# A second accumulator bank for every other pair of heads in the first chunk, and the start's step list written anew

## The chip, the cores and the metric

The kernel runs on one core of a Trainium2 chip. The metric is device time of one execution in microseconds (us); the smaller the better. Before the change three runs took 729.26, 729.31 and 729.64 us; their median is 729.31 us.

Engines are called as in the profile: PE is the matmul engine (PEld its weight loads), DVE the vector engine, ACT the scalar engine, POOL the general one, and SP the one that issues nearly all DMAs. PE writes its results to PSUM, which this kernel divides into eight banks, each a tile of up to 128 x 512 fp32 words. POOL neither reads nor writes PSUM here.

## The reference

Windowed attention with sink keys, and behind it a two-layer MLP with softplus between the layers, on B, H, S, D = 4, 8, 768, 64, with n_sink = 4, window = 128, and 512 and 2048 as the MLP's widths:

```python
scores = scale * np.matmul(q, k.transpose(0, 1, 3, 2))
keep = is_sink | in_window               # the first 4 keys, or 0 <= row - key < 128
a = softmax(np.where(keep, scores, -1e9))
x = np.matmul(a, v)                      # heads side by side: 3072 tokens x 512
h = x @ w_in                             # 512 x 2048
g = np.maximum(h, 0.0) + np.log1p(np.exp(-np.abs(h)))
return g @ w_out                         # 2048 x 512
```

## The kernel before

The 3072 tokens go through in 12 chunks of 256. A chunk has 8 attention steps, one for each head, and 8 MLP steps, one for each 256 of the 2048 columns. The MLP of a chunk runs one chunk behind its attention, so that PE has MLP matmuls to do while the other engines work on the softmax.

**Attention of one head.** `scores` (S) multiplies queries and keys into two PSUM tiles. `softmax` (T): DVE applies mask and maximum (L243, L249), ACT the exponential and the row sum (L250). `normalise` (N): DVE forms the reciprocal (L256, L257), and the engine named in the string NM scales the weights `a` (L264, or L262 on ACT). `weights_t` (W): PE transposes `a` into the PSUM tile `t`, an engine named in TH copies that to `th`, and POOL masks it twice into `pt` (L308, L311). `sink_weights` and `sink` (k, K) do the same for the sink keys of four heads at once: DVE gives `sa`, PE the tile `ts`, ACT the copy `sk`. `values` (V): PE multiplies `sk` and `pt` with the values into the PSUM tile `x` (L327, L333). `out` (O): ACT rounds `x` to `xh`, DVE takes the rest `xl` = `x` - `xh`.

In chunks 0 and 1 (`exact`) the attention is in plain fp32, and two heads share one `x` tile: the even head fills rows 0 to 63, the odd one rows 64 to 127, and `out` reads both after the odd head. The pool of `x` has one buffer, so the next pair's first matmul waits until DVE's `xl` has read the last pair's tile.

**MLP.** `up` (U) is 24 matmuls (L459), `softplus` (F), `gate` (P) and `residue` (R) form `gh` and `gl`, and `down` (D, E) adds six matmuls for each half step to two accumulators `acc0` and `acc1` (L496 to L498), each one PSUM bank.

**Weights.** They are read as 32 pieces of 128 x 512 words (`wi00` to `wo71`: layer, step, half) in the start alone, and stay. A piece needs a DMA (w), a copy of its upper bits to `upper0` or `upper1` (a; engine in WT), one DVE operation that puts the word together (c, L403), its rounded part (d; engine in WH) and its rest (l; engine in WL). The word lies in SBUF (`wt`), or, where WM has a `p`, in a PSUM bank of the accumulators that the MLP does not use yet (`word_ps`). Since POOL has no part in PSUM, the code gives such a word's rounding to ACT if WH names POOL, and its rest always to DVE.

**What sets the order.** PE and SP run their instructions in the order in which the code issues them. For the first 20 steps that is the list START, a letter and a step number for each call; from then on it is the loop over STEADY. DVE, ACT and POOL get an order from the compiler's scheduler, from the same calls. Each engine works its own queue strictly in order: an instruction that waits holds all behind it.

PSUM's eight banks are `acc` 2, `h` 2 (in chunk 0 also the scores of odd heads), `s` 2, `t` 1, `x` 1. The accumulators' two banks hold nothing until the first `down`, except for `word_ps`.

Of the kernel before, what the change touches and what calls it, by code (L numbers as in the profile page):

```python
# [841 lines left out]
Ctx.START = """
j4 w w w J0 S0 T0 G4 w S1 S2 w N0 L8 T1 T2 S3 w N1 L10 S4 W1 T3 a N2 W0 w T4 a N3 S5 k0 c c K0 a S6
w d c T5 d V0 V1 l N4 l W2 T6 w d O0 a G6 c S7 W3 O1 l N5 N6 T7 V2 a a c N7 d W4 k4 S8 a T8 O2 w V3
c S9 c O3 w w K4 d a l l W5 V4 T9 S10 W6 L12 N9 V5 O4 d T10 w l N8 O5 W7 G8 d S11 w c T11 l a V6 V7
G10 a L14 N11 N10 O6 k8 w w c W8 O7 U0 d c l a d S12 d w a w l T12 l c d K8 V8 l N12 F0 O8 c a P0 c
R0 a d a c w l w d W9 c U1 a S13 F1 d T13 c d a l a l l w P1 N13 V9 c w G12 d l D0 w w d c L16 w R1
U2 w O9 d l a W10 F2 a l w S14 c d T14 c d l P2 l W11 V10 a a U3 N14 c c w O10 p16 d a L17 F3 E0 E1
S15 d a l R2 T15 G14 D1 w E2 c a L18 d w P3 w c l d c a w S16 c l d N15 d V11 l O11 U4 k12 l a L19
W12 p17 F4 K12 a R3 T16 D2 P4 d c d l D3 a S17 l a N16 c V12 W13 d l c l p18 a U5 E3 F5 O12 R4 T17 a  # L850
c G16 W14 l P5 c V13 O13 U6 D4 E4 l S18 J16 L20 N17 l p19 F6 c T18 W15 R5 V14 d p20 U7 D5 L21 F7 d
S19 q16 P6 V15 E5 L22 O14 T19 N19 d O15 S20 N18 R6 T20 k16 W16 G18 U8 P7 R7 K16 N20 D6 F8 E6 P8 V16
O16 p21
"""


# [50 lines left out]
```

## Time and profile before

| what | value |
|---|---|
| three runs | 729.26, 729.31, 729.64 us |
| profiled execution | 731.77 us, of which 730.1 us lie between the first and the last instruction (the span) |
| PE busy | 701.6 us, 96% of the span |
| DVE, ACT, POOL busy | 579.6 (79%), 452.2 (62%), 377.5 us (52%) |
| granted PE clock over the span | 0.99 |
| DMA | 63.21 MB |

The busy share of PE in forty slices of the span is 7, 7, 8 tenths in the first three, then 9 or more until the last, which has 6. Times of single instructions are counted from the start of the span. "Idle before" is the time in which an engine had nothing running, with the instruction that ended it.

### The profile page before, as it was taken

The numbers are of one execution on the slowest core, as the hardware profiler recorded it, in microseconds if no ns is written. First come the engines' busy times: TensorE is split into PE (matmuls) and PEld (weight loads), VectorE is DVE, ScalarE is ACT, GpSimd is POOL, SyncE is SP. The second block draws the span as 40 slices with busy tenths as digits, with TensorE's granted clock in tenths as the row PEclk, the third lists the DMA queues.
The fourth block names the chain that finished last, engine by engine and source line by source line (L and its number), as shares of the span: only waits on it lengthen the run. The fifth ranks groups of instructions, "written<-read, shape, count | busy, mean of one in ns | idle before, by whom it ended". The sixth has DMA issues, their size and how long they took to land.

```text
span 730.1 us, 13819 instructions
## 1 busy us (share of the span) xinstructions
PE 701.6 (96%) x4505; PEld 622.6 (85%) x4505; DVE 579.6 (79%) x1693; ACT 452.2 (62%) x1104; POOL 377.5 (52%) x682
## 2 busy tenths in 40 slices
PE   7789999999999999999999999999999999999996
PEld 5467789988898998989899898898898898998995
DVE  6799988878988888887987987988898887864332
ACT  4579856666765766665666666665766666654331
POOL 5666486565564554664554564556555465552000
PEclk9899999999999999999999999999999999999998
DMA  9886622211411321321222222221212222100001
GB/s 308 268 316 216 182 67 74 73 53 38 118 49 48 110 64 49 106 64 46 84 64 67 77 79 68 78 76 45 86 51 79 69 76 78 58 14 1 29 1 34
DMA packets 40875, 63.21 MB, mean 87 GB/s; under 512 B 4634, under 2 KB 22362, under 8 KB 40794
## 3 DMA queue, kind: packets, MB, share of 16 engines
q1 hardware_dynamic: 40506, 61.97, 27.9%
q8 instruction: 38, 0.62, 0.4%
q14 instruction: 43, 0.35, 0.2%
q10 hardware_dynamic: 288, 0.26, 0.1%
HBM read 55.93 MB, written 6.29 MB: 85 GB/s over the span
## 4 chain that ended last, share of the span: by engine, by line
PE 73%; DVE 8%; ACT 7%; POOL 7%; issue 4%; DMA 1%; POOLq 0%; ACTq 0%
PE h L459 30%; PE acc L498 10%; PE acc L496 9%; PE acc L497 9%; PE x L333 6%; PE t L297 2%; POOL pt L308 2%; PE s L230 2%; PE s L231 2%; PE x L327 2%; POOL pt L311 2%; ACT a L250 1%; ACT mt L466 1%; ACT mt L467 1%; POOL vs L159 1%
## 5 line engine op out<-in xcount | busy, mean ns | idle before, releaser
L459 PE MATMUL h<-xh,wi 128*128 128x256 f32 x1536 | 253.6, 287 | 0.0
L459 PEld LDWEIGHTS h<-xh,wi 128*128 128x128 f32 x1536 | 211.1, 191 | 1.6 <-issue 0.5
L264 POOL TENSOR_SCALAR a<-a,rc 128x128 f32<-128x128 f32 x178 | 69.2, 401 | 186.1 <-DVE rc L257 150.4
L459 PE MATMUL h<-xl,wi 128*128 128x256 f32 x768 | 154.5, 283 | 0.0
L496 PE MATMUL acc<-wo,gh 128*128 128x512 f32 x384 | 151.7, 395 | 0.0
L498 PE MATMUL acc<-wo,gl 128*128 128x512 f32 x384 | 150.9, 393 | 0.6 <-DVE gl L56 0.6
L497 PE MATMUL acc<-wo,gh 128*128 128x512 f32 x384 | 150.6, 392 | 0.0
L459 PEld LDWEIGHTS h<-xl,wi 128*128 128x128 f32 x768 | 119.6, 192 | 0.0
L474 DVE SCALAR_TENSOR_TENSOR mt<-h,mt 128x512 f32<-128x512 f32 x96 | 66.1, 688 | 66.8 <-ACT mt L468 58.4
L466 ACT ACTIVATE mt<-h 128x512 f32<-128x512 f32 x96 | 57.1, 595 | 96.0 <-PE h L459 96.0
L250 ACT ACTIVATE a<-a,stats 128x136 f32<-128x136 f32 x192 | 76.3, 398 | 56.9 <-DVE stats L249 56.3
L498 PEld LDWEIGHTS acc<-wo,gl 128*128 128x128 f32 x384 | 72.1, 188 | 17.5 <-DVE gl L56 1.0
L496 PEld LDWEIGHTS acc<-wo,gh 128*128 128x128 f32 x384 | 72.1, 188 | 12.8 <-issue 0.3
L497 PEld LDWEIGHTS acc<-wo,gh 128*128 128x128 f32 x384 | 72.2, 188 | 9.0
L56 DVE TENSOR_TENSOR gl<-mt,gh 128x512 fp32r<-128x512 f32 x96 | 74.8, 780 | 0.3
L308 POOL TENSOR_SCALAR_AFFINE_SELECT pt<-tl 128x256 fp32r<-128x256 f32 x80 | 59.7, 746 | 27.8 <-DVE tl L56 27.7
L308 POOL TENSOR_SCALAR_AFFINE_SELECT pt<-th 128x256 fp32r<-128x256 f32 (+1 forms) x96 | 42.5, 442 | 40.2 <-ACT th L48 36.7
L467 ACT ACTIVATE mt<-mt 128x512 f32<-128x512 f32 x96 | 60.7, 633 | 3.1
L468 ACT ACTIVATE mt<-mt 128x512 f32<-128x512 f32 x96 | 60.7, 632 | 3.0
L48 ACT CAST qkh<-qk 128x656 fp32r<-128x656 f32 x80 | 59.5, 744 | 0.9 <-DMA qk<-qk 0.9
L333 PE MATMUL x<-pt,vv 128*128 128x256 f32 (+1 forms) x216 | 48.7, 328 | 8.0 <-POOL pt L311 8.0
L56 DVE TENSOR_TENSOR kl<-qk,qkh 128x400 fp32r<-128x400 f32 x80 | 53.6, 670 | 2.5
(185 smaller groups left out, 1234.7 us busy)
## 6 DMA issues: line engine op xcount, KB each, us to landing
qk<-qk SPq DMA_DIRECT2D x160, 164.0 KB, 3.1
vr<-v SPq DMA_DIRECT2D x32, 192.0 KB, 2.8
out<-o SPq DMA_DIRECT2D x24, 256.0 KB, 2.2
vr<-v SPq DMA_DIRECT2D x16, 128.0 KB, 2.3
q<-q SPq DMA_DIRECT2D x7, 256.0 KB, 5.1
k<-k SPq DMA_DIRECT2D x8, 200.0 KB, 4.1
wi00r<-w SPq DMA_DIRECT2D x1, 511.8 KB
wi01r<-w SPq DMA_DIRECT2D x1, 511.8 KB, 6.3
```

The source lines that it names most:

```text
L56: (nc.vector if eng == "V" else nc.gpsimd).tensor_tensor(out, a, b, ALU.subtract)
L250: nc.scalar.activation(a, a, AF.Exp, bias=nm, scale=-1.0, accum_out=sm[:, j : j + 1])
L264: (nc.vector if eng == "V" else nc.gpsimd).tensor_scalar(a, a, rc[:, j : j + 1], 0.0, ALU.mult, ALU.add)
L308: nc.gpsimd.affine_select(pt[:, e, :, 1], src[:], [[0, CH], [1, P]], ALU.is_ge, 0.0, base=0, channel_multiplier=-1)
L333: nc.tensor.matmul(x[:, :, o], w, pt[:, :, m], start=False, stop=n == 2, skip_group_check=True)
L459: nc.tensor.matmul(h[:, j], wt, x, start=k == 0, stop=k >= len(prods) - 2, skip_group_check=True)
L466: nc.scalar.activation(t[:], h[:], AF.Abs)
L467: nc.scalar.activation(t[:], t[:], AF.Exp, scale=-1.0)
L474: nc.vector.scalar_tensor_tensor(t[:], h[:], 0.0, t[:], ALU.max, ALU.add)
L496: nc.tensor.matmul(acc[:], gh[:, j, q], wh, start=f == 0, stop=False, skip_group_check=True)
L497: nc.tensor.matmul(acc[:], gh[:, j, q], wl, start=False, stop=False, skip_group_check=True)
L498: nc.tensor.matmul(acc[:], gl[:, j, q], wh, start=False, stop=f == 2 * FP - 1, skip_group_check=True)
```

## The change

- In chunk 0, `x` of the heads 2/3 and 6/7 (`h % 4` is 2 there when the tile is made) is written to the bank `acc0`. The heads 0/1 and 4/5 keep the bank of `x`, as does chunk 1.
- `word_ps` has one tile in the bank `acc1` in place of two in `acc0` and `acc1`, and the rule that finishes an older word before a new one is put into PSUM goes by that number.
- The strings that give operations to engines are new, and the places in WM with a `p`: wo01, wo10, wi31 and wo21, which were wi21, wo10 and wi31.
- START is a new list of the same calls.

```diff
             if h % 2 == 0:
-                self.xt = c.ps_x.tile([P, 1, CT], F32, tag="x", name=f"x{chunk}_{h}")
+                pool, tag = (c.ps_acc, "acc0") if chunk == 0 and h % 4 else (c.ps_x, "x")
+                self.xt = pool.tile([P, 1, CT], F32, tag=tag, name=f"x{chunk}_{h}")
...
             elif kind == "c" and home == "p":
-                while sum(_turn(c.WM, k) == "p" for k, _ in todo["l"] if k < o) > 1:
+                while sum(_turn(c.WM, k) == "p" for k, _ in todo["l"] if k < o) >= len(c.word_ps):
                     stage("l")(i)
...
-        c.word_ps = [c.ps_acc.tile([P, WH], I32, tag=f"acc{e}", name=f"word_ps{e}") for e in range(2)]
+        c.word_ps = [c.ps_acc.tile([P, WH], I32, tag="acc1", name="word_ps")]
...
-Ctx.NM = "PPVAPAPPPAVPPAPVP"
-Ctx.TH = "AAVVAAAAVAAAAAVVVA"
-Ctx.GH = "AAVAVPPVV"
-Ctx.WM = "sssssssppsspssssssssssssssssssss"
-Ctx.WT = "PVAVVVAAVAAAAAAVAAAAAAAAAAAPAAAP"
-Ctx.WH = "VAPAAVAAVAVAPAAAAVAAVAAAAAAAAAAP"
-Ctx.WL = "PPPVPPVVPPPVPVPPVPVPPPPVVVVVPVVP"
+Ctx.NM = "PPPAPAAPVPPPPAVVP"
+Ctx.TH = "AVVVVAAAAAAAAVVVVA"
+Ctx.GH = "AAPAAVPVV"
+Ctx.WM = "ssssspsspsspspssssssssssssssssss"
+Ctx.WT = "AVAAVAAAAAAPAAAVAAAAAAAAAAAVAAAP"
+Ctx.WH = "VAPAAVAAPAVAPAAAAVAVPAAAAAAPAAAA"
+Ctx.WL = "PPPVPPVVVPPPPVPPVPVPPPPVVVVPPVVP"
...
 Ctx.START = """
-j4 w w w J0 S0 T0 G4 w S1 S2 w N0 L8 T1 T2 S3 w N1 L10 S4 W1 T3 a N2 W0 w T4 a N3 S5 k0 c c K0 a S6
...
+w S0 j4 T0 N0 S1 J0 w T1 S2 w w w T2 S3 w G4 N1 W0 L8 w L10 S4 a T3 W1 S5 N2 T4 N3 k0 c a S6 c K0 d
...
```

In the built programs the orders differ only in the start. From PE's second transpose of chunk 2 (`t2_1`; in the trace of before at 114.89 us) all five queues hold the same instructions in the same order, and ahead of it each queue holds the same work but for what the strings move: DVE has 302 instructions there in place of 304, ACT 139 in place of 137, POOL 106 in place of 105, PE 292 as before.

Names below are the program's with a running number behind: `x0_2_417` is the `x` tile of chunk 0, heads 2/3. First PE at the second pair's values, in the program before:

```order
L297 MATMUL t0_3_391<-ident_62,a0_0_205 128x128 x2
L327 MATMUL x0_2_417<-sk0_0_325,vsf0_198 64x256
L333 MATMUL x0_2_417<-pt0_2_366,vr0_1_177 64x256
L333 MATMUL x0_2_417<-pt0_2_366,vr0_1_177 64x128
L297 MATMUL t0_4_431<-ident_62,a0_1_298 128x128 x2
L227 MATMUL s1_0_0_441<-k1_0_232,q1_0_234 128x264
L227 MATMUL s1_0_1_443<-k1_0_232,q1_0_234 128x264
L327 MATMUL x0_2_417<-sk0_0_325,vsf0_198 64x256
L333 MATMUL x0_2_417<-pt0_3_396,vr0_1_177 64x256
L333 MATMUL x0_2_417<-pt0_3_396,vr0_1_177 64x128
```

and now (one line lower in the file, hence L328 and L334):

```order
L297 MATMUL t0_3_402<-ident_62,a0_0_197 128x128 x2
L328 MATMUL x0_2_426<-sk0_0_328,vsf0_214 64x256
L334 MATMUL x0_2_426<-pt0_2_364,vr0_1_177 64x256
L334 MATMUL x0_2_426<-pt0_2_364,vr0_1_177 64x128
L227 MATMUL s1_0_0_430<-k1_0_263,q1_0_265 128x264
L227 MATMUL s1_0_1_432<-k1_0_263,q1_0_265 128x264
L297 MATMUL t0_4_436<-ident_62,a0_1_301 128x128 x2
L328 MATMUL x0_2_426<-sk0_0_328,vsf0_214 64x256
L334 MATMUL x0_2_426<-pt0_3_407,vr0_1_177 64x256
L334 MATMUL x0_2_426<-pt0_3_407,vr0_1_177 64x128
```

The place of the values is the same; the scores of chunk 1's first head have moved ahead of `t0_4`, and `x0_2` is another bank now, which the text of a row doesn't show.

POOL at the masks that these values read, before:

```order
L264 TENSOR_SCALAR a0_1_298<-a0_1_298,rc0_1_299 128x128 x2
L56 TENSOR_TENSOR wi01_346<-wt0_0_1_320,wi01_346 128x512
L308 AFFINE_SELECT pt0_2_366<-th0_2_364 128x2x128
L311 AFFINE_SELECT pt0_2_366<-th0_2_364 128x128
L52 TENSOR_SCALAR wi10_378<-wt1_0_0_337 128x512
L308 AFFINE_SELECT pt0_3_396<-th0_3_394 128x2x128
L311 AFFINE_SELECT pt0_3_396<-th0_3_394 128x128
L56 TENSOR_TENSOR wi10_378<-wt1_0_0_337,wi10_378 128x512
```

and now:

```order
L264 TENSOR_SCALAR a0_1_301<-a0_1_301,rc0_1_302 128x128 x2
L308 AFFINE_SELECT pt0_2_364<-th0_2_362 128x2x128
L311 AFFINE_SELECT pt0_2_364<-th0_2_362 128x128
L56 TENSOR_TENSOR wi01_338<-wt0_0_1_323,wi01_338 128x512
L52 TENSOR_SCALAR wi10_369<-wt1_0_0_336 128x512
L56 TENSOR_TENSOR wi10_369<-wt1_0_0_336,wi10_369 128x512
L308 AFFINE_SELECT pt0_3_407<-th0_3_405 128x2x128
L311 AFFINE_SELECT pt0_3_407<-th0_3_405 128x128
```

The mask of head 2 has moved ahead of the rest of wi01, and that of head 3 behind the rests of wi01 and wi10.

DVE where the single `word_ps` is used twice in a row, now:

```order
L404 SCALAR_TENSOR_TENSOR word_ps_187<-wi31r_479,upper1_184 128x512
L475 SCALAR_TENSOR_TENSOR mt0_0_682<-h0_0_615,mt0_0_682 128x512
L256 TENSOR_SCALAR sm1_4_656<-sm1_4_656 128x2
L257 RECIPROCAL rc1_1_655<-sm1_4_656 128x2
L404 SCALAR_TENSOR_TENSOR wt2_1_0_695<-wo20r_550,upper0_183 128x512
L56 TENSOR_TENSOR gl0_0_699<-mt0_0_682,gh0_0_689 128x512
L56 TENSOR_TENSOR wi31_702<-word_ps_187,wi31_702 128x512
L404 SCALAR_TENSOR_TENSOR word_ps_187<-wo21r_589,upper1_184 128x512
```

Before, wo21's word went to SBUF (`wt2_1_1`) and stood ahead of the rest of wi31. Now it can only be written when ACT has rounded wi31 and DVE has taken its rest.

## Rows read from the trace of the kernel before

**Rows 1.** The page's first part: busy us, share, instructions of each engine.

```profile
PE 701.6 (96%) x4505; PEld 622.6 (85%) x4505; DVE 579.6 (79%) x1693; ACT 452.2 (62%) x1104; POOL 377.5 (52%) x682
```

**Rows 2.** Busy time by stretch: PE, PEld, DVE, ACT, POOL (instructions), PE clock, DMA share, GB/s.

```profile
0.00:50.00 50.00, 37.84 (x173) 26.28 (x173) 39.34 (x162) 28.48 (x89) 31.04 (x67) 0.90 0.90 307
50.00:115.00 65.00, 62.80 (x390) 52.86 (x390) 57.85 (x141) 49.67 (x111) 42.20 (x55) 1.00 0.46 145
115.00:650.00 535.00, 527.02 (x3487) 477.21 (x3486) 451.95 (x1325) 346.41 (x856) 295.81 (x545) 1.00 0.24 70
```

**Rows 3.** Timeline of PE: start, duration, line, operation, count, idle before with releaser.

```profile
10.42 2.02 PE L227 MATMUL s<-k,q 128*128 128x264 f32 x8 [1.07 <-DVE stats L249]
...
23.62 1.12 PE L327 MATMUL x<-sk,vsf 128*64 128x256 f32 x2 [3.40 <-DVE xl L56]
...
28.33 1.12 PE L327 MATMUL x<-sk,vsf 128*64 128x256 f32 x2
...
47.22 1.12 PE L327 MATMUL x<-sk,vsf 128*64 128x256 f32 x2 [2.71 <-ACT sk L48]
```

**Rows 4.** Busy time by short stretches; the PE clock is third from the end.

```profile
23.60:25.00 1.40, 1.38 (x4) 0.79 (x5) 1.33 (x11) 0.83 (x3) 1.40 (x3) 0.50 0.78 196
...
28.00:29.00 1.00, 1.00 (x3) 0.47 (x3) 0.56 (x4) 0.00 (x0) 0.31 (x2) 0.50 1.05 374
...
49.20:50.00 0.80, 0.80 (x4) 0.27 (x3) 0.80 (x2) 0.63 (x2) 0.57 (x2) 0.50 1.05 384
```

**Rows 5.** Timeline of DVE and POOL from 20 to 24.5 us.

```profile
20.25 1.27 POOL L56 TENSOR_TENSOR wi<-wt,wi 128x512 fp32r<-128x512 f32 x1
...
20.48 1.35 DVE L50 CAST upper<-wi11r 128x512 f16<-128x512 bf16 x1
...
21.46 0.62 POOL L308 TENSOR_SCALAR_AFFINE_SELECT pt<-th 128x256 f32<-128x256 f32 x1
...
22.04 0.74 POOL L311 TENSOR_SCALAR_AFFINE_SELECT pt<-th 128x128 f32<-128x128 f32 x1
...
22.77 0.61 POOL L52 TENSOR_SCALAR wi<-wt 128x512 fp32r<-128x512 f32 x1
...
23.16 0.41 DVE L56 TENSOR_TENSOR xl<-x,xh 128x256 fp32r<-128x256 f32 x1
23.34 0.40 POOL L308 TENSOR_SCALAR_AFFINE_SELECT pt<-th 128x256 f32<-128x256 f32 x1
...
23.70 0.29 POOL L311 TENSOR_SCALAR_AFFINE_SELECT pt<-th 128x128 f32<-128x128 f32 x1
...
23.96 1.26 POOL L56 TENSOR_TENSOR wi<-wt,wi 128x512 fp32r<-128x512 f32 x1
```

**Rows 6.** Timeline of DVE at 12 us: scaling of head 2's weights.

```profile
12.75 0.48 DVE L264 TENSOR_SCALAR a<-a,rc 128x128 f32<-128x128 f32 x2
```

**Rows 7.** Timeline at 45 us: DVE's rounding of wo10, chunk 1's fifth head, ACT's sink copy.

```profile
43.98 0.68 DVE L50 CAST wo<-word_ps 128x512 fp32r<-128x512 f32 x1
...
45.30 0.48 DVE L243 COPY_PREDICATED s<-diag,s 128x128 f32<-128x128 int32 x2
...
46.83 0.34 ACT L48 COPY sk<-ts 32x256 f32<-32x256 f32 x1
```

**Rows 8.** Timelines of POOL, DVE and ACT: one word in PSUM from write to last read.

```profile
46.13 0.69 DVE L403 SCALAR_TENSOR_TENSOR wt<-wi30r,upper 128x512 int32<-128x512 int32 x1
...
47.36 1.27 POOL L56 TENSOR_TENSOR wi<-wt,wi 128x512 fp32r<-128x512 f32 x1 [1.59 <-DVE sm L256]
47.47 1.72 DVE L403 SCALAR_TENSOR_TENSOR word_ps<-wi31r,upper 128x512 int32<-128x512 int32 x1
...
50.98 0.58 ACT L48 CAST wi<-word_ps 128x512 fp32r<-128x512 f32 x1
...
52.10 0.68 DVE L56 TENSOR_TENSOR wi<-word_ps,wi 128x512 fp32r<-128x512 f32 x1
```

More of the change, by code (lines that the diff above doesn't have):

```diff
@@ L841 @@
+Ctx.WL = "PPPVPPVVVPPPPVPPVPVPPPPVVVVPPVVP"
 Ctx.STEADY = ("kWRqpUKFSTDPNVOE", "kqWRpSDKTUFNPVEO")
 Ctx.START = """
-j4 w w w J0 S0 T0 G4 w S1 S2 w N0 L8 T1 T2 S3 w N1 L10 S4 W1 T3 a N2 W0 w T4 a N3 S5 k0 c c K0 a S6
-w d c T5 d V0 V1 l N4 l W2 T6 w d O0 a G6 c S7 W3 O1 l N5 N6 T7 V2 a a c N7 d W4 k4 S8 a T8 O2 w V3
-c S9 c O3 w w K4 d a l l W5 V4 T9 S10 W6 L12 N9 V5 O4 d T10 w l N8 O5 W7 G8 d S11 w c T11 l a V6 V7
-G10 a L14 N11 N10 O6 k8 w w c W8 O7 U0 d c l a d S12 d w a w l T12 l c d K8 V8 l N12 F0 O8 c a P0 c
@@ L847 @@
[L847 to L851, printed above, removed]
@@ L852 @@
-S19 q16 P6 V15 E5 L22 O14 T19 N19 d O15 S20 N18 R6 T20 k16 W16 G18 U8 P7 R7 K16 N20 D6 F8 E6 P8 V16
-O16 p21
+w S0 j4 T0 N0 S1 J0 w T1 S2 w w w T2 S3 w G4 N1 W0 L8 w L10 S4 a T3 W1 S5 N2 T4 N3 k0 c a S6 c K0 d
+a w c d V0 l V1 T5 N4 W2 l a d T6 O0 S7 c l w O1 T7 N6 W3 a a w G6 N5 c N7 V2 S8 d W4 k4 a T8 c V3
+O2 c O3 K4 S9 d w l w a l W5 T9 V4 d O4 S10 N9 W6 T10 L12 V5 l N8 O5 a W7 w S11 c G8 d T11 N10 l N11
+V6 V7 L14 w O6 c w a W8 c k8 d O7 d w U0 G10 a d l w S12 l a T12 c d l K8 V8 w l F0 c a P0 N12 c O8
@@ new lines @@
+R0 a d l a w U1 W9 c d F1 d a l S13 c T13 w d c d a l w N13 w P1 a w l w V9 c U2 c L16 w l D0 d G12
+O9 a d w R1 l W10 S14 a c F2 d T14 l c d l P2 a c V10 U3 W11 w E0 N14 a S15 d c p16 E1 a a R2 l O10
+L17 D1 w F3 T15 d c E2 a P3 G14 d w L18 c c d w a c d w l l N15 w d V11 l l O11 k12 S16 l W12 p17 a
+U4 K12 R3 F4 T16 a D2 c c L19 d D3 l S17 P4 d a a N16 G16 d l W13 l V12 c U5 l p18 R4 O12 a E3 F5
+T17 d a c P5 U6 W14 D4 V13 E4 c S18 c L20 J16 l N17 l l O13 p19 F6 W15 R5 P6 U7 d T18 D5 p20 V14 S19
@@ L854 @@
+q16 F7 L21 W16 V15 E5 T19 O14 L22 R6 N18 S20 N19 d G18 O15 k16 T20 P7 R7 U8 K16 N20 F8 D6 V16 E6 P8
+p21 O16
 """
```

## The prediction

> **What bounds the kernel now.** I read the page's first part first: PE is busy for 701.6 of 730.1 us [rows 1], so the kernel is as long as PE's work and its gaps. Next the busy time by stretches [rows 2]: from 50 to 650 us PE lacks 2.2 us of 65 and 8 us of 535, in the first 50 us it lacks 12.2 of 50, and there its mean clock is 0.90. All five queues hold the same work in the same order behind 114.89 us, and PE holds the same work ahead of it. So the change's effect is what PE idles, or runs slowly, less or more in the first 115 us.
>
> The timeline of PE shows where the 12.2 us lie. The two large gaps are 3.40 us ahead of 23.62, ended by DVE's `xl`, and 2.71 us ahead of 47.22, ended by ACT's sink copy [rows 3]. The rest is the first 2 us and gaps of 1.1 us and less. Both large gaps are followed by the lower clock: 0.50 granted, that is 1.2 of 2.4 GHz, from 23.6 to 29 and from 47.2 to 50 us [rows 4]. That is 5.4 + 2.8 = 8.2 us at half speed, so 4.1 us lost. The two gaps and what follows them cost 3.40 + 2.71 + 4.1 = 10.2 us, and that is the most this change can be worth there.
>
> **The change part by part.** *The first gap.* PE could do the values of head 2 (the matmuls at 23.62) once POOL's mask `pt0_2` is there, but waits until DVE has taken `xl` out of the only `x` bank, at 23.16 + 0.41 = 23.57 [rows 3, 5]. With `x0_2` in a bank of its own that wait is gone, and the mask is late next: in the trace it ends at 22.04 + 0.74 = 22.78. It also moves: it stood behind the 1.27 us of wi01's rest, which began at 20.25, and now stands ahead of it. So POOL begins it where that rest began. Its two parts took 23.99 - 23.34 = 0.65 us for head 3 and 22.78 - 21.46 = 1.32 for head 2 [rows 5]; I take 0.95, nearly the middle, with both as bounds.
>
> One thing ahead of it costs time. Head 1's copy `th0_1` goes from ACT to DVE and stands on DVE right behind head 3's softmax, while PE now transposes head 1 only behind the scores of head 4. DVE waits there; queued behind it are the row sums, head 4's softmax and the sink weights, which PE waits for. In return DVE loses the scaling of head 2 (0.48, [rows 6]) and a copy of upper bits there. I put this at 0.5 us later for everything behind it, with bounds of -0.4 (the 0.48 of scaling counts in full) and 1.1 (a whole gap as at 10.42, [rows 3]).
>
> So the mask ends at 20.25 + 0.5 + 0.95 = 21.7, and PE, which was done with what stands ahead at 23.62 - 3.40 = 20.2, now at 20.7, waits 1.0 us. Head 3's mask has moved back behind wi01's rest and wi10: 21.7 + 1.27 + 0.61 + 1.26 + 0.65 = 25.5 [rows 5]. What PE has to do between the two took 28.33 - 23.62 = 4.7 us at half speed [rows 3, 4], so 2.4 at full, and it waits 25.5 - 21.7 - 2.4 = 1.4 us more, then starts head 3's values at 25.5 in place of 28.33. Two gaps of 1.0 and 1.4 stand for one of 3.40: 1.0 us is won, 0.5 of it lost to the later front.
>
> *The clock.* A gap of 1.07 us left it at the higher level in the first 16 us, one of 3.40 did not [rows 3, 4]. The new gaps lie nearer to the first, so I take the higher clock: 5.4 / 2 = 2.7 us won. Bounds: 0 and 2.7.
>
> *The second gap.* Before head 0 of chunk 1 can be multiplied, the sink copy has to leave ACT, and ACT's queue has it behind head 4's exponential, which waits for DVE. DVE began that head at 45.30, behind wo10's rounding and rest, and the copy began 1.5 us later [rows 7]. The rounding of wo10 (0.68) goes to ACT, so DVE comes 0.68 us sooner after PE's scores and the gap falls to 2.71 - 0.68 = 2.0. Bounds: 1.5 (the part that is behind DVE's start) and 2.71. It is the shorter gap of the two in the trace that cost the clock, and 2.0 is not far below it; I take the 1.4 us as won, with 0 as the other bound.
>
> *What runs beside.* By the strings DVE loses two copies of upper bits, a `gh` and one rounding, and gains two `th`: two operations less on balance, of at most 0.68 us [rows 7]. ACT gets two more on balance, at 0.58 for one [rows 8], POOL three roundings for a copy. DVE does 57.85 us in the 65 us up to 115 and ACT 49.67 [rows 2], so the cover is 7 us on DVE and 15 on ACT. All of it sits in orders that follow PE's, which keeps the lead it has at 50 us only if DVE has it too. DVE's own idle time at the start hung on the same slow scores and `x` tiles, so I let it come along. SP's list moves as well: four weight pieces, wi11 to wo01, are issued ahead of chunk 1's first keys. These keys are needed right behind the values of head 2, some 2 us earlier than now; I cost that at nothing, with 1 us as its bound, since DMAs were busy for 0.90 of the first 50 us [rows 2].
>
> *Stalls between DVE and POOL.* The same word operation took 0.69 us alone and 1.72 beside a two-input operation of POOL, whose end at 47.36 + 1.27 = 48.63 it outlasted by 0.56 [rows 8]. One such stall more on the path costs 1.03; I take 0.7 for that chance, with 0 and 2.1 (two) as bounds.
>
> The page "SBUF — State Buffer" of the Trainium skill, section "Who interferes with whom", says that a POOL instruction reading SBUF and a DVE one with two SBUF inputs exclude each other for a whole instruction. By that rule POOL's three new roundings (gh0_2, wo40, wi71) each hold DVE for their full length between 50 and 95 us; the row of 1.72 us agrees with the rule.
>
> *The sum.* 1.0 - 0.5 + 2.7 + (2.71 - 2.0 = 0.7) + 1.4 - 0.7 = 4.6 us. I leave the 2.2 us that PE lacks from 50 to 115 us as they are. The profiled execution took 731.77 us, so it would take 727.2; the median of the runs is 2.46 below the profiled one, which gives 724.7. I forecast 724.8 us. With every bound at its worst the sum is 1.0 - 0.4 (the longer mask) - 1.1 - 1.0 (the keys) - 2.1 = -3.6, which is 732.9; at its best, 1.0 + 0.3 (the shorter mask) + 0.4 + 2.7 + 1.2 + 1.4 = 7.0, which is 722.3.
>
> **The rivals.**
>
> *The wait changes its name.* PE waits for masks and exponentials as long as it did for `xl`, since DVE, which feeds them, was nearly always busy after 8 us. For it: DVE is busy for 39.34 us of the first 50, most of it behind 7 us. Against it: POOL's own order moves the mask by 1.27 us whatever DVE does. Price: the 1.0 of the first gap and the clock there are gone, and 0.7 of the second stays: 728.6, no change.
>
> *The clock falls all the same.* PE's work from 20.7 to 26.5 is thin, with 2.4 us of gaps, and 2.0 at the second place. For it: both gaps above 2.7 were followed by 0.50. Against it: single gaps of 1.0 to 1.1 us weren't. If only the first stretch is slow, the gain is 4.6 - 2.7 = 1.9 (727.4); if both are, 0.5 (728.8).
>
> *POOL holds DVE.* The three roundings at 0.61 each [rows 5] lie between 50 and 95 us, where DVE has little idle time: 1.8 us lost, gain 2.8, 726.5. For it: the row of 1.72. Against it: DVE gives up a `gh` and a rounding there. The skill's page named above is what speaks for the full 0.61 each.
>
> *The single word bank makes it slower.* In the trace a word stands in its bank from 47.47 to 52.78, 5.3 us, until ACT (50.98) and DVE (52.10) have read it [rows 8]; with two banks the next one didn't wait. Now there are four such words in one bank, wo21's write stands right behind the rest of wi31, and DVE's whole queue behind it: masks, scores' maxima, gates. Each time that ACT rounds later than DVE arrives, DVE stops, and PE's first matmul into `acc1` has to wait for wo21's rest. ACT has more to do. At 1.2 us a word the 4.6 are gone, from 1.6 a word it is slower by more than 0.2%; at 2, which I take as its price, it is 8 - 4.6 = 3.4 slower, 732.7. Against it: the first `down` now comes after PE's third `up`, 24 matmuls later, and between word and rest of wi31 DVE has five other operations.
>
> **How the numbers follow.** Changes within 0.2%, 1.46 us, can't be told from none. Forecast, a gain of 3 to 6.5 us: 0.58. More than that: 0.09. POOL holds DVE: 0.08. The clock falls: 0.09, half of it beyond 1.46 us. The wait changes its name: 0.09. The word bank: 0.07, slower. Faster: 0.58 + 0.09 + 0.08 + 0.05 = 0.80; same: 0.04 + 0.09 = 0.13; slower 0.07. The range of 721.9 to 728.9 takes in all but the word bank, the very best gains (beyond the bounds, where the 2.2 us shrink as well) and a little of the unchanged cases, some 0.13 together. The forecast's own range is 722.8 to 726.3.
>
> **What would show it.** Right: the values of head 2 start near 21.7 and wait for `pt`, not for `xl`; the clock is 1.00 from 20 to 40 us; the sink copy's gap is near 2 us; `t2_1` on PE starts near 110.3 in place of 114.89, and from there on nothing differs. Wrong: a gap of 3 us or a clock of 0.50 near 25 us; `word_ps` as what DVE waits for; PE gaps between 50 and 115 us that add up to more than 2.2.

## The result, and the profile after

The changed kernel takes 731.52 us (median of 12 runs, 730.79 to 734.65), beside 729.90 for the kernel before on the same chip: ratio 1.0021, 95% interval 1.0011 to 1.0030. It is slower by 0.2%, 1.6 us, at the edge of what can be told from no change. A gain of 4.6 us was forecast. The profiled execution took 732.06 us, with a span of 730.4. The profiled execution of the kernel before, 731.77 us, took longer than any of the 12 runs behind 729.90 (the longest 731.58), so the two traces lie only 0.3 us apart.

The page's first part, which answers to [rows 1]: DVE has two instructions fewer and is busy 2.0 us longer.

```profile
PE 701.0 (96%) x4505; PEld 621.6 (85%) x4505; DVE 581.6 (80%) x1691; ACT 453.6 (62%) x1106; POOL 379.6 (52%) x682
```

Busy time by stretches, with the columns of [rows 2]:

```profile
0.00:50.00 50.00, 41.00 (x210) 29.42 (x210) 41.18 (x166) 34.86 (x100) 34.13 (x71) 1.00 0.91 316
50.00:115.00 65.00, 58.92 (x352) 48.62 (x351) 57.31 (x136) 45.56 (x103) 39.99 (x52) 0.97 0.47 138
115.00:650.00 535.00, 526.94 (x3485) 477.13 (x3484) 452.42 (x1325) 345.58 (x855) 296.83 (x545) 1.00 0.24 70
```

Beside the trace of before, the first 50 us gained what was forecast: PE does 210 instructions in place of 173, lacks 9.0 us in place of 12.2, and its clock is 1.00 in place of 0.90. From 50 to 115 us the gain goes: PE lacks 6.1 us in place of 2.2, the clock's mean is 0.97 in place of 1.00, and 352 instructions stand for 390. Behind 115 us nothing differs.

PE's timeline (start, duration, line, operation, idle before and what ended it) has, instead of the gaps of [rows 3], these:

```profile
21.02 0.86 PE L334 MATMUL x<-pt,vr 128*64 128x256 f32 x4 [0.60 <-POOL pt L311]
...
25.03 0.86 PE L334 MATMUL x<-pt,vr 128*64 128x256 f32 x4 [0.59 <-POOL pt L311]
...
42.50 0.65 PE L328 MATMUL x<-sk,vsf 128*64 128x256 f32 x2 [2.12 <-ACT sk L48]
...
56.62 0.65 PE L328 MATMUL x<-sk,vsf 128*64 128x256 f32 x2 [0.86 <-DVE xl L56]
58.63 1.44 PE L334 MATMUL x<-pt,vr 128*64 128x128 f32 x6 [1.36 <-POOL pt L311]
...
70.53 0.50 PE L499 MATMUL acc<-wo,gl 128*128 128x512 f32 x1 [0.54 <-DVE gl L56]
78.53 0.38 PE L281 MATMUL ts<-ident,sa 128*32 128x128 f32 x2 [1.58 <-DVE sa L269]
...
101.83 0.50 PE L499 MATMUL acc<-wo,gl 128*128 128x512 f32 x1 [1.56 <-DVE gl L56]
```

The first three rows are the forecast's: the values of heads 2 and 3 wait for masks, 0.6 us each, where 3.40 us of waiting for `xl` stood, and the sink copy's gap is 2.12. The last five add up to 5.9 us; the trace of before has four in their place, of 0.52 to 0.62 us, 2.2 in all. By stretches (columns as above) the clock that answers to [rows 4] is at the higher level behind the gap of 2.12 us, and at the lower one, 0.50, behind the gaps of 0.86 and 1.36:

```profile
42.50:44.00 1.50, 1.50 (x9) 1.01 (x9) 0.92 (x2) 1.44 (x3) 1.11 (x1) 1.00 1.03 377
...
60.00:61.00 1.00, 1.00 (x5) 1.00 (x5) 0.97 (x2) 1.00 (x5) 0.26 (x1) 0.50 0.61 240
61.00:62.00 1.00, 1.00 (x7) 1.00 (x6) 1.00 (x3) 0.42 (x1) 0.00 (x0) 0.50 0.25 98
...
63.00:64.00 1.00, 1.00 (x10) 1.00 (x9) 0.93 (x4) 0.00 (x0) 0.54 (x1) 1.00 0.00 0
```

PE's start of the same work in the traces of before and after, and in that of an experiment below (the hybrid), in us:

| PE begins | before | after | hybrid |
|---|---|---|---|
| second `up` of chunk 0 (U1) | 50.25 | 43.94 | 43.97 |
| fourth `up` (U3) | 64.44 | 60.00 | 58.57 |
| chunk 1's second sink transpose (`ts1_1`) | 79.69 | 78.53 | 73.83 |
| `t2_1`, from where all is equal | 114.89 | 115.19 | 109.14 |

The lead is 6.3 us at U1, 4.4 at U3, 1.2 at `ts1_1` and -0.3 at `t2_1`. Part of the 6.3 belongs to the trace of before, not to the kernel. An experiment below, the kernel before without six `gl`, has the same list and the same work up to U1, and in its trace the clock falls once in the first 50 us and not behind the sink copy's gap. Its PE row at that gap, and its first 50 us by the columns of [rows 2]:

```profile
45.64 0.65 PE L327 MATMUL x<-sk,vsf 128*64 128x256 f32 x2 [2.06 <-ACT sk L48]
```

```profile
0.00:50.00 50.00, 38.53 (x196) 28.22 (x197) 40.49 (x164) 30.23 (x92) 32.80 (x68) 0.97 0.90 318
```

There U1 begins at 47.28. Over that execution, which took 1.2 us less than its kernel's median, the changed kernel leads by 3.3 us. The hybrid starts U1 where the changed kernel does and is 6.05 us ahead of it at `t2_1`, whatever the kernel before does. So there is one question: why does the changed kernel not keep a lead that it has at 44 us?

DVE's timeline of the changed kernel shows where DVE, which is busy for 44.22 us of the 49 from 45 to 94 (46.22 before), stands still, and one long operation at the end:

```profile
55.45 0.69 DVE L404 SCALAR_TENSOR_TENSOR wt<-wo31r,upper 128x512 int32<-128x512 int32 x1 [0.48 <-issue]
...
65.74 0.69 DVE L404 SCALAR_TENSOR_TENSOR wt<-wo41r,upper 128x512 int32<-128x512 int32 x1 [1.45 <-issue]
...
75.49 1.03 DVE L404 SCALAR_TENSOR_TENSOR wt<-wo51r,upper 128x512 int32<-128x512 int32 x1 [0.68 <-ACT upper L48]
...
85.81 0.69 DVE L404 SCALAR_TENSOR_TENSOR wt<-wo60r,upper 128x512 int32<-128x512 int32 x1 [1.09 <-ACT upper L48]
...
98.50 3.27 DVE L56 TENSOR_TENSOR gl<-mt,gh 128x512 fp32r<-128x512 f32 x1
```

Each of the four is a word that waits for upper bits that are late on ACT; the first two are put down to "issue", but the upper bits end on ACT just ahead of them (those of wo41 at 64.86 + 0.79 = 65.65). The timeline of ACT around the second one:

```profile
60.66 0.76 ACT L48 CAST upper<-wo40r 128x512 f16<-128x512 bf16 x1
64.59 0.37 ACT L48 COPY th<-t 128x256 f32<-128x256 f32 x1 [3.17 <-PE t L297]
64.86 0.79 ACT L48 CAST upper<-wo41r 128x512 f16<-128x512 bf16 x1
```

ACT waits 3.17 us for PE's transpose of chunk 1's head 3 (W11), with the upper bits of wo41 queued behind it, and DVE waits for those.

The two gaps near 57 us have the same look. PE transposes chunk 1's head 2 at 54.49 in the changed kernel and at 54.63 in the hybrid, but ACT's copy `th`, which POOL's mask needs, comes at 56.64 in the one and at 55.81 in the other,

```profile
56.64 0.36 ACT L48 COPY th<-t 128x256 f32<-128x256 f32 x1
```

and DVE's `xl`, which PE's gap of 0.86 us waits for, at 56.14 and 55.29.

### The profile page after: what moved, and what is told of

Its sections match the earlier page's. It is cut to its first block, busy times and chain, and to the rows that moved or that the text cites. A ratio compares the mean times of both kernels' runs of the same rounds, so it can differ in the third digit from the quotient of the medians.

```text
span 730.4 us, 13832 instructions
## 1 busy us (share of the span) xinstructions
PE 701.0 (96%) x4505; PEld 621.6 (85%) x4505; DVE 581.6 (80%) x1691; ACT 453.6 (62%) x1106; POOL 379.6 (52%) x682
## 4 chain that ended last, share of the span: by engine, by line
PE 67%; DVE 13%; ACT 7%; POOL 7%; issue 4%; DMA 2%; SPq 0%; POOLq 0%; ACTq 0%; DVEq 0%
PE h L460 28%; PE acc L499 9%; PE acc L497 9%; PE acc L498 9%; PE x L334 5%; PE t L297 2%; POOL pt L308 2%; PE s L230 2%; PE s L231 2%; DVE gl L56 2%; ACT a L250 1%; POOL pt L311 1%; DVE s L243 1%; ACT mt L467 1%; DVE kl L56 1%
## 5 line engine op out<-in xcount | busy, mean ns | idle before, releaser
L264 POOL TENSOR_SCALAR a<-a,rc 128x128 f32<-128x128 f32 x178 | 67.4, 392 | 183.7 <-DVE rc L257 147.4
L56 DVE TENSOR_TENSOR gl<-mt,gh 128x512 fp32r<-128x512 f32 x96 | 79.5, 828 | 0.2
L334 PE MATMUL x<-pt,vv 128*128 128x256 f32 (+1 forms) x216 | 48.7, 328 | 8.1 <-POOL pt L311 8.1
```

The costliest lines, as they stand in the source:

```text
L56: (nc.vector if eng == "V" else nc.gpsimd).tensor_tensor(out, a, b, ALU.subtract)
L264: (nc.vector if eng == "V" else nc.gpsimd).tensor_scalar(a, a, rc[:, j : j + 1], 0.0, ALU.mult, ALU.add)
```

## The experiments

Three theories: **A**, W11, which the new list puts behind V10 and U3, holds up ACT and through it DVE. **B**, POOL's new operations hold DVE's two-input ones. **C**, DVE's work sets the pace up to some 95 us, so a lead that PE alone has can't be kept. Later a fourth, **D**: the changed list's order behind U1 as a whole.

| kernel | ratio to before | 95% |
|---|---|---|
| changed kernel | 1.0021 | 1.0011 to 1.0030 |
| W11 back ahead of V10 | 1.0022 | 1.0013 to 1.0031 |
| three roundings taken from POOL | 1.0044 | 1.0030 to 1.0057 |
| changed, without six `gl` | 0.9970 | 0.9957 to 0.9982 |
| before, without six `gl` | 0.9990 | 0.9981 to 0.9999 |
| banks alone, old list | 1.0107 | 1.0091 to 1.0123 |
| hybrid: order of before behind U1 | 0.9954 | 0.9938 to 0.9970 |
| five operations from DVE to ACT | 1.0052 | 1.0034 to 1.0071 |
| changed list, the hybrid's strings | 1.0012 | 0.9996 to 1.0027 |
| hybrid list, changed strings | 0.9973 | 0.9962 to 0.9984 |
| hybrid from V10 on | 0.9980 | 0.9970 to 0.9989 |
| hybrid, K8 ahead of T12 | 0.9940 | 0.9927 to 0.9953 |
| wo71's rest from POOL to DVE | 1.0011 | 1.0000 to 1.0022 |
| single word bank alone, old list | 1.0124 | 1.0107 to 1.0140 |
| x bank, one word, old list | 1.0014 | 1.0002 to 1.0026 |

**W11 back (theory A).**

```diff
-... P2 a c V10 U3 W11 w E0 N14 ...
+... P2 a c W11 V10 U3 w E0 N14 ...
```

> The changed kernel (1.0021 of before) with one token moved: the transposes of chunk 1's head 3 (W11) stand again ahead of that chunk's head 2's values and the third step's up product, as before. Theory A (the lead of 6.3 us at 44 us is lost because this transpose now sits behind V10 on PE, ACT stands still 3.2 us for it at 64.6 and DVE 1.5 us behind ACT): 2 to 3 us faster than the changed kernel, ratio to before about 0.998 to 0.999. Theory B (POOL's three new roundings hold DVE): no change, 1.002. Theory C (DVE has as much left to do as before, so PE must give its lead back wherever it first needs DVE): at most 0.5 us, 1.001 to 1.002; the wait shows under another name.

No change against the changed kernel in the medians, so A falls as the whole cause. The wait did move: in DVE's timeline the 1.45 us at 65.74 are gone, and two others are there, behind upper bits that are as late as before.

```profile
54.12 0.69 DVE L404 SCALAR_TENSOR_TENSOR wt<-wo30r,upper 128x512 int32<-128x512 int32 x1 [0.82 <-issue]
55.85 0.69 DVE L404 SCALAR_TENSOR_TENSOR wt<-wo31r,upper 128x512 int32<-128x512 int32 x1 [1.04 <-ACT upper L48]
```

The clock blurs this result. Its stretches show the lower level behind the sink copy's gap, which is 2.10 us here and 2.12 in the changed kernel, where it didn't fall:

```profile
42.50:44.00 1.50, 1.50 (x6) 1.11 (x7) 0.86 (x2) 1.44 (x3) 1.17 (x1) 0.63 1.02 373
44.00:45.00 1.00, 1.00 (x5) 0.47 (x4) 0.77 (x2) 0.90 (x3) 0.49 (x1) 0.50 1.04 405
```

On the other hand it isn't at 0.50 near 60 us any more: the gaps of 0.86 and 1.36 us there are 0.62 and 0.56. In these two traces one loss of the clock, some 1.7 us, stands for the other. The one behind the sink copy's gap lies ahead of the token that was moved, so what W11 is worth by itself stays open.

**POOL's three roundings given back (theory B).**

```diff
-Ctx.GH = "AAPAAVPVV"
-Ctx.WH = "VAPAAVAAPAVAPAAAAVAVPAAAAAAPAAAA"
+Ctx.GH = "AAVAAVPVV"
+Ctx.WH = "VAPAAVAAPAVAPAAAAVAVVAAAAAAAAAAA"
```

> The changed kernel with POOL's three new roundings (gh of step 2, wo40, wi71) given back to the engines that had them before (DVE, DVE, ACT). Theory B: DVE's stretched two-input operations near 62 to 69 and 83 to 90 us go back to 0.7 us; 1.8 to 3 us faster than the changed kernel, ratio to before 0.998 to 1.000. Theory A: no change, 1.002. Theory C: DVE gets two operations of 0.6 to 0.7 us more and loses about as much in stretching; within 0.7 us of the changed kernel either way, 1.001 to 1.003.

Slower than the changed kernel, 1.0044 to 1.0021. DVE's three `kl` (the rests of rounded keys) between 45 and 94 us take 605 ns in place of 934 in the mean, but that comes from one of them, and in the changed kernel it stands beside POOL's rest of a weight piece, not beside a rounding:

```profile
66.88 1.47 POOL L56 TENSOR_TENSOR wi<-wt,wi 128x512 fp32r<-128x512 f32 x1
67.21 1.56 DVE L56 TENSOR_TENSOR kl<-qk,qkh 128x400 fp32r<-128x400 f32 x1
```

The three roundings took longer themselves, 0.98, 1.13 and 0.99 us on POOL for 0.61 in [rows 5]. DVE's words and rest beside them kept their 0.68 to 0.69; only two short operations were lengthened, by some 0.7 us together (`sm` at 62.98, 0.59 us for 0.15, and `qkh` at 66.46, 0.72 for 0.42). The Trainium skill's page "SBUF — State Buffer" (section "Who interferes with whom") says that a POOL instruction that reads SBUF and a DVE one with two SBUF inputs contend, and that the order of issue decides which of them waits. The trace agrees: POOL's rounding of 1.13 us began at 65.78, behind DVE's word at 65.74. So B falls for these three. Why the time is longer isn't shown by this run: PE lacks 6.0 us from 50 to 115 us, as in the changed kernel (6.1), and the clock's means, 0.97 in the first 50 us and 0.96 from 70 to 115, cost some 3.3 us, where the changed kernel loses 1.7 near 60 us. That difference is as large as the one between the two kernels.

**Six `gl` left out (theory C).** In chunk 0, steps 1 to 6, `gh` is multiplied once more in place of `gl`: PE's work is the same, DVE's is six operations less.

```diff
         _, t = self.t.pop(s)
+        if chunk == 0 and 1 <= s <= 6:
+            self.g[s].append(self.g[s][0])
+            return
         gl = ...
```

> The changed kernel without DVE's six subtractions gl of steps 1 to 6 of chunk 0 (the rounded gate is multiplied once more in its place: PE's work is the same, that part of the result is left out). They take 6 x 0.7 to 3.3 us of DVE between 56 and 99 us, some 7 us. Theory C: PE keeps most of its lead, 3 to 5 us faster than the changed kernel, ratio to before 0.995 to 0.998. Theory A: ACT still waits for the late transpose, at most 1 us faster, 1.001. Theory B: the stalls move to the next two-input operations; 1 to 2 us faster, 0.999 to 1.001.

> The kernel before without the same six subtractions of DVE. PE lacks only 2.2 us between 50 and 115 us there, about 0.5 of it ended by gl. All theories: 0 to 1 us faster, ratio to before 0.9985 to 1.000. If it gains 3 us or more, DVE held PE before as well and theory C says nothing about the change.

The changed kernel gains 3.7 us (1.0021 to 0.9970, of 730), the kernel before 0.7. As C expects: before, DVE had just enough time; behind a PE that comes earlier it hasn't. PE's waits for `gl` at 70.53 and 101.83 are gone with the operations, and that for `sa` is smaller:

```profile
77.18 0.38 PE L281 MATMUL ts<-ident,sa 128*32 128x128 f32 x2 [0.92 <-DVE sa L269]
```

The two waits ahead of 60 us are as they were (0.85 and 1.37), with the low clock behind them.

**The hybrid (C against D).** The changed kernel's list and strings up to U1; behind it, whatever is left in the order and on the engines of before.

```diff
-Ctx.GH = "AAPAAVPVV"
+Ctx.GH = "AAVAVPPVV"
...
-R0 a d l a w U1 W9 c d F1 d a l S13 c T13 w d c d a l w N13 w P1 a w l w V9 c U2 ...
-... T14 l c d l P2 a c V10 U3 W11 w E0 N14 a S15 d c p16 E1 a a R2 l O10 ...
+R0 a d l a w U1 c w d W9 c a S13 F1 d T13 c d a l a l l w P1 N13 V9 c w G12 ...
+... T14 c d l P2 l W11 V10 a a U3 N14 c c w O10 p16 d a L17 F3 E0 E1 ...
```

> The changed kernel's list and strings up to the second up product (PE at 44 us), and from there the steps that are left in the order, and on the engines, of the kernel before. PE's front of 0 to 50 us is the changed one with its lead of 6.3 us. Theory C: DVE is only some 2 us ahead there, so at most that remains: 0 to 2 us faster than before, ratio 0.997 to 1.000. The rival that the changed list's later part is at fault (its order holds up one engine after another, whichever token one looks at): the lead stays, 3 to 6 us faster than before, ratio 0.992 to 0.996.

0.9954: 3.4 us faster than before, nearly 5 faster than the changed kernel. The lead stays (table above), beyond what I took C to allow. PE's timeline from 42 to 115 us has these gaps over 0.3 us and no others:

```profile
42.52 0.65 PE L328 MATMUL x<-sk,vsf 128*64 128x256 f32 x2 [2.10 <-ACT sk L48]
49.25 1.08 PE L334 MATMUL x<-pt,vr 128*64 128x128 f32 x6 [0.47 <-POOL pt L311]
56.22 0.44 PE L297 MATMUL t<-ident,a 128*128 128x128 f32 x2 [0.32 <-ACT th L48]
57.56 1.08 PE L334 MATMUL x<-pt,vr 128*64 128x128 f32 x6 [0.32 <-POOL pt L311]
73.83 0.39 PE L281 MATMUL ts<-ident,sa 128*32 128x128 f32 x2 [0.52 <-ACT th L48]
76.75 0.50 PE L499 MATMUL acc<-wo,gl 128*128 128x512 f32 x1 [0.66 <-DVE gl L56]
```

and by stretches the clock holds, and DVE is busy as never before:

```profile
45.00:94.00 49.00, 46.70 (x286) 38.28 (x284) 47.24 (x112) 42.76 (x94) 33.71 (x39) 1.00 0.66 208
50.00:115.00 65.00, 63.18 (x395) 53.62 (x394) 59.28 (x148) 49.72 (x114) 44.39 (x58) 1.00 0.48 142
```

DVE has no wait over 0.4 us between 45 and 94 us: no word waits for upper bits, since the list now has the copies (`a`) a step earlier against U3 and the scores. DVE does set the pace there, 96% busy, but it can do so at a rate that keeps the lead, if nothing makes it stand still. So D holds, and C in part: the order behind U1 loses the lead, and with DVE 96% busy there is little idle time in which a wait of DVE could be made good. That each such wait counts in full is argued, not shown.

**Five operations from DVE to ACT.**

```diff
-Ctx.TH = "AVVVVAAAAAAAAVVVVA"
-Ctx.GH = "AAPAAVPVV"
-Ctx.WT = "AVAAVAAAAAAPAAAVAAAAAAAAAAAVAAAP"
-Ctx.WH = "VAPAAVAAPAVAPAAAAVAVPAAAAAAPAAAA"
+Ctx.TH = "AVVVVAAAAAAAAAVVVA"
+Ctx.GH = "AAPAAAPVV"
+Ctx.WT = "AVAAVAAAAAAPAAAVAAAAAAAAAAAAAAAP"
+Ctx.WH = "VAPAAVAAPAVAPAAAAAAAPAAAAAAPAAAA"
```

> The changed kernel with five single-input operations of DVE between 50 and 95 us given to ACT: the roundings of wo31 and wi51, the rounding of gate 5, the copy th of chunk 1's head 5, the upper bits of wi71; nothing is left out. They are 5 x 0.4 to 0.7, some 2.5 us of DVE; ACT idles some 19 us of those 65. Theory C: 1 to 2.5 us faster than the changed kernel, ratio to before 0.999 to 1.001. If ACT's queue is the bound instead: the same or slower than the changed kernel, 1.002 to 1.004.

Slower still, 1.0052, against C alone. In DVE's timeline the wait for the upper bits has grown:

```profile
67.44 0.69 DVE L404 SCALAR_TENSOR_TENSOR wt<-wo41r,upper 128x512 int32<-128x512 int32 x1 [3.40 <-issue]
```

The same word as at 65.74 in the changed kernel now waits 3.40 us: DVE comes earlier, the upper bits come later. Less work on DVE brought nothing where DVE waits in order for ACT. The upper bits are late because ACT waits for W11's transposes, 3.78 us in place of 3.17, and PE comes to those 1.7 us later, behind a longer stretch at the lower clock:

```profile
60.00:70.00 10.00, 10.00 (x48) 8.81 (x47) 5.81 (x11) 6.19 (x15) 4.02 (x6) 0.73 0.13 46
```

The clock's mean there is 0.73 in place of 0.87, and 0.93 in place of 0.96 in the ten us ahead, 1.7 us in all. That is most of the 2.3 us by which this run is slower, so it doesn't show that ACT's longer queue is what costs the time.

**Order or engines.** The two halves of the hybrid's edit, each alone: first the changed list with the hybrid's strings,

```diff
-Ctx.NM = "PPPAPAAPVPPPPAVVP"
-Ctx.GH = "AAPAAVPVV"
-Ctx.WM = "ssssspsspsspspssssssssssssssssss"
-Ctx.WT = "AVAAVAAAAAAPAAAVAAAAAAAAAAAVAAAP"
-Ctx.WH = "VAPAAVAAPAVAPAAAAVAVPAAAAAAPAAAA"
-Ctx.WL = "PPPVPPVVVPPPPVPPVPVPPPPVVVVPPVVP"
+Ctx.NM = "PPPAPAAPVPPPPAPVP"
+Ctx.GH = "AAVAVPPVV"
+Ctx.WM = "ssssspsspsspssssssssssssssssssss"
+Ctx.WT = "AVAAVAAAAAAPAAAVAAAAAAAAAAAPAAAP"
+Ctx.WH = "VAPAAVAAPAVAPAAAAVAAVAAAAAAAAAAP"
+Ctx.WL = "PPPVPPVVVPPPPVPPVPVPPPPVVVVVPVVP"
```

> The changed list, whole, with the hybrid's strings: from the second up product on every rounding, copy and subtraction of the first 20 steps is on the engine that it had in the kernel before. If the order behind U1 is what loses the lead: as the changed kernel, ratio to before 1.000 to 1.004. If the engines' shares (DVE too full, POOL holding it) lose it: as the hybrid, 0.994 to 0.997.

then the hybrid's list with the changed kernel's strings:

```diff
-... T14 l c d l P2 a c V10 U3 W11 w E0 N14 a S15 d c p16 E1 a a R2 l O10 ...
+... T14 c d l P2 l W11 V10 a a U3 N14 c c w O10 p16 d a L17 F3 E0 E1 ...
```

> The hybrid's list (changed up to the second up product, then the order of before) with the changed kernel's strings throughout. Order theory: DVE's waits for upper bits on ACT stay away, as the hybrid, 0.994 to 0.997. Engines' shares theory: as the changed kernel, 1.000 to 1.004. Between the two, 0.997 to 1.000, if both have a part.

The strings alone bring nothing that can be told (1.0012, its interval across 1 and overlapping the changed kernel's), the list alone 0.0048 of the 0.0067 between changed kernel and hybrid, with intervals apart. So the order has the greater part. The trace of the strings alone loses 3.4 us to the clock from 50 to 70 us (means 0.95 and 0.71), twice as much as the changed kernel's, so a gain by the strings may be hidden there. DVE's mean of one `gl` from 45 to 94 us goes 1122 ns (changed), 898 (list back), 716 (both back), which speaks for a part of the engines' shares in the rest. That isn't shown: the intervals of the list alone and of the hybrid overlap, and in the trace of the list alone the clock falls behind the sink copy's gap (2.11 us), which the hybrid's doesn't.

**The place.** As the hybrid, but the changed list runs on to V10.

```diff
-... P2 a c V10 U3 W11 w E0 N14 a S15 d c p16 E1 a a ...
+... P2 a c V10 w l W11 a U3 N14 c w O10 p16 d a L17 ...
```

> As the hybrid, but the changed list and strings run on to the values of chunk 1's head 2 (PE at 57 us), with W11 behind them, and the order of before only from there. If the loss sits in what is queued between 44 and 57 us (late upper bits on ACT, the transposes of head 3 behind V10 and U3): as the changed kernel, 1.000 to 1.003. If it is spread evenly up to 103 us: half of it, 0.997 to 1.000. If it lies behind that point: as the hybrid, 0.994 to 0.997.

0.9980, about three fifths of the way from the changed kernel to the hybrid. PE's gaps of 0.85 at 56.72 and 1.37 at 58.74 and the low clock behind them are those of the changed kernel; those at 78.53 (now 0.52) and 101.83 (gone) aren't there. So the loss has two parts: what is queued ahead of V10, and what comes behind it.

**wo71's rest off POOL.**

```diff
-Ctx.WL = "PPPVPPVVVPPPPVPPVPVPPPPVVVVPPVVP"
+Ctx.WL = "PPPVPPVVVPPPPVPPVPVPPPPVVVVPPVVV"
```

> The changed kernel with the last weight subtraction (the rest of wo71) on DVE in place of POOL. If POOL's 1.25 us of it hold DVE's gl of step 6 (3.27 us at 98.5 in the changed kernel), that gl falls to 2 us or less, PE's wait of 1.56 us ahead of 101.83 goes, and since DVE gets 0.7 us more the gain is 0.5 to 1.3 us: ratio to before 1.0003 to 1.0015. If the wait comes from DVE's place in its queue and not from POOL: the same or 0.7 us slower, 1.002 to 1.003.

1.0011, a gain of 0.7 us; the interval overlaps the changed kernel's, so the time alone would not show it. The timelines do: first DVE's `gl`, which begins 1.5 us later, since DVE now has the rest as well, but takes 0.68 us in place of 3.27,

```profile
100.01 0.68 DVE L56 TENSOR_TENSOR gl<-mt,gh 128x512 fp32r<-128x512 f32 x1
```

and PE's gap behind it, 0.42 in place of 1.56:

```profile
100.75 0.50 PE L499 MATMUL acc<-wo,gl 128*128 128x512 f32 x1 [0.42 <-DVE gl L56]
```

So the third place is POOL's doing, by an operation that POOL had in the kernel before too; there it didn't fall on a `gl` that PE waits for.

**The banks with the old list.** Both banks as in the change, with the list and strings of before.

```diff
+                pool, tag = (c.ps_acc, "acc0") if chunk == 0 and h % 4 else (c.ps_x, "x")
+                self.xt = pool.tile([P, 1, CT], F32, tag=tag, name=f"x{chunk}_{h}")
...
-        c.word_ps = [c.ps_acc.tile([P, WH], I32, tag=f"acc{e}", name=f"word_ps{e}") for e in range(2)]
+        c.word_ps = [c.ps_acc.tile([P, WH], I32, tag="acc1", name="word_ps")]
```

> The kernel before with the new bank for x of heads 2 and 6 and the single word bank, but with its own list and its own strings. Theory C (DVE's work sets the pace up to some 100 us): the wait of 3.40 us for xl goes, the mask is next, so PE's gap there shrinks to about 2.6 us, but DVE does the same work; 0 to 1 us faster than before, ratio 0.999 to 1.000. The prediction's own view (a lead of PE at 30 us stays): the gap's 0.8 us and, if the clock holds, 2.7 us more, ratio 0.995 to 0.999. If the single word bank costs something with this list, where three words stand close together (wi21, wi31, wo10), above 1.000.

1.0107, 8 us slower, beyond all that was expected. The next two take it apart: the word bank alone (only the last line of that diff and the rule that goes with it), and the x bank with one word.

```diff
-Ctx.WM = "sssssssppsspssssssssssssssssssss"
+Ctx.WM = "ssssssssssspssssssssssssssssssss"
```

> The kernel before with one word bank in place of two, and nothing else (x stays in one bank). If the word bank is what made the bank change with the old list 1.1% slower: 1.008 to 1.014, with PE's long waits for ACT's sink copy (near 48 us) and transposed weights (near 66 us). If that came from the x bank: 0.999 to 1.002.

> The bank change with the list of before, but only one word (wi31) goes through the single word bank; wi21 and wo10 are written to the ordinary buffer. If the word bank was at fault: PE's waits of 4.96 and 4.14 us go, ratio 0.997 to 1.000, which is then what the x bank alone brings with the old list. If the x bank was at fault: still 1.008 or more.

It is the word bank, 1.0124. A word has to be finished before the next may be put there, so the list pulls the rests of wi21 and wo10 ahead, and DVE does a word and a rounding more (wi30's) before chunk 1's head 4. That head's softmax begins on DVE at 47.36 in place of 45.30 [rows 7]:

```profile
47.36 0.48 DVE L243 COPY_PREDICATED s<-diag,s 128x128 f32<-128x128 int32 x2
...
49.99 0.69 DVE L56 TENSOR_TENSOR wi<-word_ps,wi 128x512 fp32r<-128x512 f32 x1 [0.65 <-ACT wi L48]
```

and PE's timeline has gaps of 5 and 4 us:

```profile
50.27 1.05 PE L327 MATMUL x<-sk,vsf 128*64 128x256 f32 x2 [4.96 <-ACT sk L48]
68.37 0.69 PE L297 MATMUL t<-ident,a 128*128 128x128 f32 x2 [3.84 <-ACT th L48]
```

The clock has a part in these 9 us: its means, 0.93 in the first 50 us and 0.92 from 50 to 115, cost some 8.7 us, where those of [rows 2] cost 5.0.

The x bank with one word is 1.0014; two words go to SBUF in it as well, so it isn't the x bank by itself. PE's timeline there: the wait for `xl` became one for the mask, and the sink copy's gap grew from 2.71 to 4.08 us.

```profile
22.76 0.86 PE L334 MATMUL x<-pt,vr 128*64 128x256 f32 x4 [2.05 <-POOL pt L311]
...
46.13 1.11 PE L328 MATMUL x<-sk,vsf 128*64 128x256 f32 x2 [4.08 <-ACT sk L48]
```

**One gap more.** The hybrid with chunk 1's sink product and copy ahead of head 4's softmax.

```diff
-... l w S12 l a T12 c d l K8 V8 w l F0 ...
+... l w S12 l a K8 T12 c d l V8 w l F0 ...
```

> The hybrid with one token moved: chunk 1's first sink product and its copy on ACT (K8) ahead of head 4's softmax (T12), so the copy no longer stands behind that head's exponentials on ACT. PE's gap of 2.1 us ahead of V8 at 42.5 us falls below 1 us. If DVE sets the pace from there on: no change against the hybrid, 0.995 to 0.997. If PE keeps the gain: 1 to 2 us more, 0.992 to 0.995.

0.9940, the fastest kernel run; its interval and the hybrid's overlap. In PE's timeline the sink copy's gap is 1.2 us smaller and the next one, for a mask, 1.0 larger, so that `t2_1` starts at 108.87, 0.3 earlier than in the hybrid:

```profile
41.23 0.65 PE L328 MATMUL x<-sk,vsf 128*64 128x256 f32 x2 [0.87 <-ACT sk L48]
48.98 1.08 PE L334 MATMUL x<-pt,vr 128*64 128x128 f32 x6 [1.48 <-POOL pt L311]
```

So the gap that was closed came back in great part at PE's next wait. It is ACT that holds it there: the mask needs the copy `th`, which ACT, without idle time ahead of it, begins at 46.81, 1.2 us behind PE's transposes at 45.65.

## Why the prediction was wrong

**The front, terms 1.0 - 0.5 + 2.7 + 0.7 + 1.4: right against the trace of before, and low.** The values of head 2 wait for `pt` and start at 21.02 (forecast 21.7), head 3's at 25.03 (25.5), the sink gap is 2.12 (2.0), and the clock is 1.00 throughout. They add up to 5.3; PE's lead at U1 over the trace of before is 6.3. The 0.5 for a later front did not come: the two gaps are 0.6 each, not 1.0 and 1.4.

**The step that failed** is the one behind it: that the orders of the other engines "follow PE's", that DVE's idle time could "come along", and that the 2.2 us that PE lacks from 50 to 115 us stay "as they are". They are 6.1 us, and the low clock near 60 us costs 1.7 more (0.04 of the ten us from 50 and 0.13 of those from 60). I costed the new list behind 50 us by its counts of operations on DVE, ACT and POOL, and by 7 us of idle time as their cover. The sign that would show it wrong, gaps there of more than 2.2 us, came. The runs show that cover is no measure here: DVE idles hardly more from 50 to 115 us than before (7.7 us to 7.2), but at words whose upper bits the list issues late on ACT, ahead of operations that PE waits for. With the order of before behind U1 the lead is 5.75 us at `t2_1`, and the gain is 3.4 us by the ratio, 95% from 2.2 to 4.5: of the 4.6 of the sum, 3.4 lie in the front and were given back by the list. I had compared the two orders at three places, all ahead of 48 us in the changed kernel, and not where a list that was re-ordered throughout differs for 50 us more.

**A second step: the clock's loss was counted twice.** The sum takes the 4.1 us at the low clock from one execution of the kernel before, and then goes from 731.77 to the median by the same 2.46 us as before the change. But that execution lost more to the clock than most, 0.990 over the span where most others of the kernel before have 0.993 to 0.997, and the trace without six `gl` shows the same list losing it once in the first 50 us, not twice. So part of the 4.1 was in the 2.46 already. The changed kernel's profiled execution lies 0.54 us above its median, not 2.46. In the traces the hybrid is 4.9 us shorter than the kernel before, in the medians 3.4. Of the 6.7 us between forecast and result, 4.9 are the lead given back (4.6 forecast, 0.3 slower from trace to trace), and the other 1.9 come from here.

**Stalls between DVE and POOL, 0.7 with 2.1 at most: too small.** The five `gl` between 45 and 94 us alone take 5.6 us, where they took 3.6 before the change; and the one at 98.50 takes 2.6 more than 0.68. But the rival that built on it named the three roundings, and these were not what DVE's long operations stood beside.

**The clock.** The changed kernel's front kept the higher level, as forecast, but by luck: its reason, the length of one gap, did not hold (below). "Clock falls all the same" did not happen in the stretches it named, but near 60 us, for 1.7 us.

**The single word bank.** Not what made the changed kernel slower: no PE wait there is for such a word, and DVE's only one is 0.34 us for wi31's rounding, at 46.80. Its price, 8 us for four words that DVE stops for, is near the 9 us that it costs with the old list, by luck: there it is three words, and the time goes because work of DVE is pulled ahead of a head's softmax, and by the clock. That the changed kernel pays little for the bank because its four words are spread out is my reading; no run here has the new list with two banks.

**The wait changes its name.** In the first 50 us it didn't. With the x bank and the old list it did: 3.40 us for `xl` became 2.05 for the mask, the sink gap grew by 1.4, and nothing was won.

A slip that changes nothing in the sum: the operations that DVE loses are put at 0.68 us at most, but the copy of upper bits in [rows 5] took 1.35.

What stays open: where the last us of the lead goes (6.6 are lost, 3.9 in gaps and 1.7 by the clock), which of the moved calls ahead of V10 make the gaps of 0.86 and 1.36 us at 57 and 59 us (they shrink with W11 back, but there PE comes later), and why the hybrid, 5.75 us ahead at `t2_1`, is 4.9 shorter in its span.
